# Linear attention and a Fourier feed-forward block on one core: single operations take other places in a plan's line, and the first queries are loaded ahead of the keys

## The chip, the core and the metric

The kernel runs on one core of a Trainium2 chip. The core has five engines that run side by side, each through its own queue in order: TensorE (PE in the profile) multiplies matrices out of SBUF into PSUM, VectorE (DVE) and ScalarE (ACT) read and write both memories, GpSimd (POOL) works on SBUF, and SyncE (SP) here does little but issue transfers (DMA). They wait for one another with semaphores. An instruction that waits holds up everything behind it on its engine.

The metric is the time of one execution on the device in microseconds. The kernel before takes 1024.65 us, the median of three runs between 1022.66 and 1026.61.

## The reference

Everything is fp32. B = 8 batches, H = 8 heads, S = 576 tokens, D = 64 per head, so 512 per token.

```python
kv  = einsum('bhsd,bhse->bhde', k, v)
out = einsum('bhsd,bhde->bhse', q, kv)
x   = out / sqrt(mean(out * out, -1) + 1e-6) * g_norm      # then heads side by side: (8, 576, 512)

mixed = real(fft(fft(x, axis=1), axis=2))
u  = x + mixed
un = (u - mean(u)) / sqrt(var(u) + 1e-6)                   # over the 512
out = u + maximum(un @ w_ch1, 0) @ w_ch2                   # 512 -> 2048 -> 512
```

The two weight matrices are given as 64-bit floats.

## The kernel before

**Stages.** For each batch, keys and values are multiplied (`ps_k`, line 590, copied to `kvt`), the queries are turned by matmuls against an identity (`ps_q`, lines 660 and 666, copied to `fq`), and queries times `kvt` give the attention output (`ps_o`, line 691; for batch 0 line 747, a second time with `kvg`, which is `kvt` times the gain `gb`). Squares are summed, a root gives the norm, and the rows are folded (`ab`, `xe`, `xh`, `xl`), since the real part of the Fourier transform needs only sums and differences of mirrored rows and columns. Two more products with constant matrices are the transform: `ps_f` over the sequence (lines 901 and 913, constants `cs`) and `ps_f` over the channels (line 955, constants `cd`). The result is mixed into `x`, turned (`ps_t`, line 1053) and kept as `unTh` and `unTl`.

**Precision.** A matmul at full rate takes a rounded form of fp32. So each factor is split into a high and a low part, and a product is three matmuls: high by high, low by high, high by low. The 64-bit weights are brought to this form on the chip: one ACT operation, five DVE steps and a sum (`ps_a`, `wp`, `wa`, lines 362 to 379 and 1109), then, for the first matrix, the mean over its rows by a matmul (`ps_w`, line 393), its subtraction on DVE (line 402), and the high and low parts.

**Feed-forward.** The 4608 tokens are nine blocks of 512; the 2048 inner columns are 16 parts of 128. `ps_h` (line 435) is a block times a part of the first matrix, `acc` (line 452) adds up the second product. Three parts of the weights are ready early, so blocks of the batches that are finished can start while later batches still go through the attention; partial sums go to DRAM and come back.

**What sets the order.** Each piece of work is entered in a plan with an engine, a cost in ns, a rank and what it needs. The planner walks through a modelled time: whenever an engine comes free it gives it the ready operation of lowest rank, if the buffers it asks for are free in their rings. The order in which the planner emits is the order on each engine's queue. Ranks are ten times the batch plus a stage (keys 0, queries 1, output 2, ... turns 7); feed-forward work has ranks from 1000. When nothing else is to be had, PE gets spare matmuls (`ps_s`, line 507), which multiply constants and whose result nobody reads. As long as no feed-forward work has begun, the planner also prefers them over waiting when PE has had few columns in its last 3.4 us.

Of the kernel before, what the change touches and what calls it, by code (L numbers as in the profile page):

```python
# [55 lines left out]
class Plan:  # L56
# [205 lines left out]
def kernel(  # L262
# [14 lines left out]
    nc = tc.nc  # L277
# [241 lines left out]
    def plan_dft(part, dst, src, n, r, key):  # L519
        size = src.shape[-2] * src.shape[-1]  # L520
        raw = ring("x", one, [P, 2 * DM], "draw")
        hi = dst[:, part, 0].rearrange("p t c -> p (t c)")
        lo = dst[:, part, 1].rearrange("p t c -> p (t c)")
        flat = src[part].rearrange("p t c -> p (t c)")
        ld = []
        for lo_, hi_ in ((0, n - n % 16), (n - n % 16, n)):
            if lo_ < hi_:
                ld.append(dma(
                    3 * (hi_ - lo_), r,
                    lambda lo_=lo_, hi_=hi_: nc.sync.dma_start(raw.t[lo_:hi_, :size], flat[lo_:hi_]),  # L530
                    kv_loaded, [raw],
                ))
        b = op("ACT", 950 if key == "s" else 620, r, lambda: nc.scalar.activation(hi, raw.t[:n, :size], AF.Copy), ld, [raw])
        c = op(
            "DVE", 1060 if key == "s" else 680, r,
            lambda: nc.vector.tensor_tensor(lo, raw.t[:n, :size], hi.bitcast(F32), ALU.subtract),
            [b], [raw], port=True,
        )
        dft[key, part] = c

    last_qkv = []

    def plan_kv(b):
# [7 lines left out]
        for pr in range(NPAIR):  # L551
# [3 lines left out]
            for c, src, kr in (("k", k, rest[0]), ("v", v, rest[1])):  # L555
                on = dict(eng="ACT") if b == 0 and c == "v" else {}
                start = nc.scalar.dma_start if on else nc.sync.dma_start
                if b == 0 and pr == NPAIR - 1:
                    main = Buf("h", lambda c=c: h_tile(c + "h").bitcast(F32).rearrange(
                        "p (h j d) -> p h j d", h=2, j=4  # L560
                    ))
                else:
                    main = Buf("kv", lambda c=c: qkv.tile(
                        [P, 2, 4, D], F32, name=c + "m", tag="m", bufs=RINGS["kv"]
                    ))
                ts.append(main)
                ld.append(dma(
                    256, rank(b, KV),
                    lambda main=main, src=src, hs=hs, start=start: start(
                        main.t.rearrange("p h j d -> p h (j d)"),  # L570
                        src[b, hs, : 4 * P].rearrange("h (p j) d -> p h (j d)", j=4),
                    ),
                    bufs=[main], **on,
                ))
                if pr == 0:
                    lds.append(dma(
                        128, rank(b, KV),
                        lambda kr=kr, src=src, start=start: start(
                            kr.t, src[b, :, 4 * P :].rearrange("h p d -> p h d")
                        ),  # L580
                        bufs=[kr], rate=150, **on,
                    ))
# [34 lines left out]
    def plan_q_load(b, side):  # L617
# [16 lines left out]

        ld = [dma(576, rank(b, QT), load, bufs=[qt], rate=290 if wide else 150)]
        if not side:
            ld.append(dma(
                2, rank(b, QT),
                lambda: nc.sync.dma_start(rows_of(qt.t[TR : TR + 1])[:, 0], q[b : b + 1, :, 0, :]),
                bufs=[qt],  # L640
            ))
        return qt, ld

    def plan_q(b, side, j, qt, ld):

        n = TR + 1 if side == 0 and j == 0 else TR
        fq = ring("fq", qkv, [P, NPAIR, TR + 1], "fq")
        done = []
# [31 lines left out]
    def plan_out(b, t, fqs, done, kvt, x, ss):  # L680
# [17 lines left out]

        r = rank(b, OUT)
        a = op("PE", 1500, r, mm, done, [kvt, x, ss] + pss + fqs)  # L700
        last_qkv.append(a)
        cs_, ds = [], []
        for s in range(2):
# [3 lines left out]

            c = op("ACT", 594, r - D1, og, [a], [pss[s], x])
            q_ = op(
# [11 lines left out]
            cs_.append(c)  # L721
        gs = []
        for side in range(2):
            def scale(side=side):
# [112 lines left out]
    def plan_fold(b, t, x, y_done, yp, gs, ms=None):  # L837
        n = rows[t]
        if ms and t == 0:
# [34 lines left out]
        def even(s):  # L874
            def go():
                o, a = two_of(xe), two_of(ab)
                nc.gpsimd.tensor_tensor(o[:, s], a[:, 0], a[:, 1], ALU.subtract if s else ALU.add)  # L877
# [4 lines left out]
        e = [op("POOL", 750, r, even(s), [f], [ab, xe]) for s in range(2)]  # L882
        h = op("ACT", 640, r, lambda: nc.scalar.activation(xhl.t[0][:n], two_of(xe), AF.Copy), e, [xe, xhl])

        def low():
            nc.gpsimd.tensor_tensor(
                xhl.t[1][:n], two_of(xe), xhl.t[0][:n].bitcast(F32), ALU.subtract
            )

        return xhl, op("POOL", 1270, r, low, [h], [xe, xhl]), z  # L890

# [52 lines left out]
    def plan_chn(b, t, x, pt, dones):  # L944
# [3 lines left out]
        for part in range(2):  # L948
# [126 lines left out]
    def plan_w(which, f, ring_, pool, r, after=(), r_load=None, slow=False, late_=False):  # L1075
# [19 lines left out]
        early = ring_ == "wA"  # L1095
        away = slow or early and which == 1
        a = dma(512, r if r_load is None else r_load, lambda: w_load(which, f, raw.t), after, [raw])
        d = op("ACT", 643, r, lambda: w_clear(raw.t, ps.t), [a], [raw, ps] + held, wait=SLACK if FILL <= r < 2 * FILL else 0)
# [101 lines left out]
    zeros = []  # L1200
    for b in range(B):
        begin = len(plan.ops)
        kvt, kvt_done, kv_loaded, kvg = plan_kv(b)
        xs = [ring("x", one, [P, 2 * DM], "x") for _ in range(3)]
        reds, gs, fqs = [], {}, {}
        for side in range(2):
            qt, loaded = plan_q_load(b, side)
            for j in range(3):
                fqs[side, 2 - j if side else j] = plan_q(b, side, j, qt, loaded)
        if b:  # L1210
# [9 lines left out]
        muls = {}  # L1220
        for t in (2, 1, 0) if b == 0 else range(3):
            pair = [fqs[side, t] for side in range(2)]
            if b == 0:
# [7 lines left out]
            )  # L1231
            reds += d
        y, yp = plan_y(b, ss, reds) if b else (None, None)
        if b == 0:
# [4 lines left out]
        xhl, lows = [None] * 3, [None] * 3  # L1239
        for t in (2, 1, 0) if b == 0 else range(3):  # L1240
            xhl[t], lows[t], z = plan_fold(b, t, xs[t], y, yp, gs.get(t), muls.get(t))
            zeros.append(z)
        gate_seq = muls.get(0, [])
        pt = Buf("pt", lambda: [one.tile([P, 2, 2, NS], F32R, name=f"pt{i}") for i in range(2)])
        pts = [plan_seq(b, grp, xhl, pt, lows) for grp in range(4)]
        for t in (2, 1, 0) if b == 0 else range(3):
            plan_chn(b, t, xs[t], pt, pts)
# [55 lines left out]

    for j in range(NBLK):
        plan_early(j, unTs[j], turned[j])


# [10 lines left out]
    for f in range(NA, F1):  # L1318
        for which in (1, 2):
            plan_w(which, f, "wB", lambda: wB1[0], FILL + f, [swapped], slow=(which == 1))  # L1320

    def close():
# [105 lines left out]
    def plan_late():  # L1428
        unT, unT_in = {}, {}
        for j in early[:2]:  # L1430
            unT[j], unT_in[j] = unTs[j], []
        begun = {}
# [158 lines left out]
```

## Time and profile before

| | |
|---|---|
| median of three runs | 1024.65 us |
| the profiled execution | 1019.38 us |
| its span, first to last instruction | 1017.6 us |
| mean granted TensorE clock | 0.992 |
| PE busy | 1005.8 us (99%) |
| DVE, ACT, POOL busy | 474.4, 325.6, 311.6 us |
| spare matmuls on PE | 84, 25.6 us |

The profile is of one execution. A row of the timeline gives start, length, engine, line, operation and `out<-in`; a row of the chain of waits gives start, length and what ran; both are in us from the span's start. An entry in square brackets is the engine's idle time before the row and what ended it. PE rows count each fp32 matmul of the short kinds as two instructions, so `x16` of one pass through the program may stand as `x32`. The granted clock is 1 at full speed and 0.5 at half.

### The profile page before, as it was taken

What the parts mean: (1) busy time and instruction counts of PE and PEld (TensorE: products, weight loads), DVE (VectorE), ACT (ScalarE), POOL (GpSimd) and SP (SyncE); (2) the same over time, 40 slices, a digit from 0 to 9 for tenths busy, and PEclk for the clock granted to TensorE, in tenths of its full rate; (3) what the DMA queues carried; (4) which work ended last, traced back from release to release, by engine and by line L of the source; (5) the groups of instructions that cost most, each with busy time, mean ns of one, the idle gap of its engine ahead of it and who ended that gap; (6) DMA issues with size and microseconds to landing.
All of it is one profiled execution on the core that took longest, in us unless ns stands there. A gap on an engine that the chain in (4) does not pass through costs nothing.

```text
span 1017.6 us, 15655 instructions
## 1 busy us (share of the span) xinstructions
PE 1005.8 (99%) x6208; PEld 846.9 (83%) x6208; DVE 474.4 (47%) x855; ACT 325.6 (32%) x651; POOL 311.6 (31%) x320
## 2 busy tenths in 40 slices
PE   7999999999999999999999999999999999999998
PEld 6898899889888788888888888888888888888886
DVE  3868674654676657988931313131221221311312
ACT  1566565655644433433312121121121121121110
POOL 0346976665664211224343232211030020020010
PEclk7999999999999999999999999999999999999999
DMA  9969885773435844668162524320310400500201
GB/s 245 228 188 263 210 245 166 218 214 118 172 105 186 294 167 166 226 212 299 34 243 60 189 93 156 114 93 21 142 65 11 176 21 1 186 21 0 104 1 42
DMA packets 103629, 144.95 MB, mean 142 GB/s; under 512 B 42638, under 2 KB 70338, under 8 KB 98436
## 3 DMA queue, kind: packets, MB, share of 16 engines
q1 hardware_dynamic: 94836, 127.04, 39.4%
q10 hardware_dynamic: 6800, 10.62, 2.9%
q0 software_dynamic: 1920, 6.29, 2.1%
q8 instruction: 49, 0.80, 0.3%
q14 instruction: 24, 0.20, 0.1%
HBM read 92.52 MB, written 51.40 MB: 141 GB/s over the span
## 4 chain that ended last, share of the span: by engine, by line
PE 90%; DMA 5%; DVE 3%; ACT 1%; issue 1%; ACTq 0%; SPq 0%; DVEq 0%
PE ps_h L435 37%; PE acc L452 36%; PE ps_o L691 3%; PE ps_f L955 3%; PE ps_f L901 3%; PE ps_k L590 3%; DMA vm<-in_v_dram 2%; DMA part_scr<-part 2%; PE ps_t L1053 1%; PE ps_q L666 1%; PE ps_s L507 1%; DMA raw<-in_moe_w_ch_dram 1%; PE ps_q L660 1%; DMA km<-in_k_dram 1%; PE ps_f L913 0%
## 5 line engine op out<-in xcount | busy, mean ns | idle before, releaser
L452 PE MATMUL acc<-w,hh 128*128 128x512 f32 x1152 | 357.9, 392 | 0.0
L435 PE MATMUL ps_h<-unTh,w 128*128 128x512 f32 x1152 | 356.2, 390 | 0.0
L447 DVE SCALAR_TENSOR_TENSOR hl<-ps_h,hh 128x512 fp32r<-128x512 f32 x144 | 99.2, 689 | 367.2 <-ACT hh L444 366.5
L435 PEld LDWEIGHTS ps_h<-unTh,w 128*128 128x128 f32 x1152 | 214.8, 188 | 43.8
L452 PEld LDWEIGHTS acc<-w,hh 128*128 128x128 f32 x1152 | 213.9, 188 | 43.6
L444 ACT ACTIVATE hh<-ps_h 128x512 fp32r<-128x512 f32 x144 | 86.0, 598 | 474.6 <-PE ps_h L435 459.7
L452 PE MATMUL acc<-w,hl 128*128 128x512 f32 x576 | 224.7, 390 | 0.5 <-DVE hl L447 0.4
L435 PE MATMUL ps_h<-unTl,w 128*128 128x512 f32 x576 | 224.2, 389 | 0.0
L1423 POOL TENSOR_TENSOR uu<-uu,up 128x512 f32<-128x512 f32 x36 | 45.4, 1297 | 314.4 <-DVE hl L447 228.0
L452 PEld LDWEIGHTS acc<-w,hl 128*128 128x128 f32 x576 | 108.1, 188 | 24.1 <-DVE hl L447 1.3
L435 PEld LDWEIGHTS ps_h<-unTl,w 128*128 128x128 f32 x576 | 108.1, 188 | 22.6
L726 POOL TENSOR_TENSOR x<-x,gb 96x512 f32<-96x512 f32 (+1 forms) x42 | 54.5, 1316 | 53.2 <-ACT x L706 50.5
L1131 POOL TENSOR_TENSOR w<-wap,w 128x512 fp32r<-128x512 f32 x18 | 24.1, 1342 | 92.7 <-ACT w L1126 92.6
L715 DVE TENSOR_REDUCE ss<-ps_o 96x8 f32<-96x512 f32 (+1 forms) x42 | 28.8, 687 | 34.8 <-ACT ps_o L711 29.4
L1468 DVE SCALAR_TENSOR_TENSOR uu<-acc,rs_yb,uu 128x512 f32<-128x512 f32 x36 | 25.2, 744 | 41.7 <-PE acc L452 41.7
L877 POOL TENSOR_TENSOR xe<-ab 96x256 f32<-96x256 f32 (+1 forms) x46 | 35.2, 787 | 22.4 <-DVE ab L870 21.2
L1365 POOL TENSOR_TENSOR up<-up 128x512 f32<-128x512 f32 x16 | 20.5, 1293 | 65.1 <-DMA up<-next_scr 64.9
L1065 DVE TENSOR_TENSOR unTl<-ps_t,unTh 128x384 fp32r<-128x384 f32 (+14 forms) x80 | 33.4, 481 | 8.0 <-ACT unTh L1062 8.0
L955 PE MATMUL ps_f<-cd,pt 128*96 128x258 f32 (+1 forms) x288 | 35.9, 282 | 0.0
L955 PEld LDWEIGHTS ps_f<-cd,pt 128*96 128x96 f32 (+1 forms) x288 | 34.8, 162 | 0.7
L901 PE MATMUL ps_f<-cs,xh 97*128 97x290 f32 (+1 forms) x168 | 34.3, 299 | 0.0
L691 PEld LDWEIGHTS ps_o<-kvt,fq 64*96 64x96 f32 (+1 forms) x672 | 30.7, 162 | 4.2 <-issue 3.2
(135 smaller groups left out, 1045.7 us busy)
## 6 DMA issues: line engine op xcount, KB each, us to landing
raw<-in_moe_w_ch_dram SPq DMA_DIRECT2D x32, 512.0 KB
unTh<-unT_scr SPq DMA_DIRECT2D x11, 1024.0 KB
unTl<-unT_scr SPq DMA_DIRECT2D x11, 1024.0 KB
qt<-in_q_dram SPq DMA_DIRECT2D x16, 576.0 KB
unT_scr<-unTh SPq DMA_DIRECT2D x9, 1024.0 KB
unT_scr<-unTl SPq DMA_DIRECT2D x9, 1024.0 KB
part_scr<-part ACTq DMA_DIRECT2D x36, 256.0 KB
up<-part_scr SPq DMA_DIRECT2D x36, 256.0 KB
```

The source lines that it names most:

```text
L435: nc.tensor.matmul(ps, w[c][:, kc * P : (kc + 1) * P], unT[a][:, kc, :], start=(kc == 0 and n == 0), stop=(kc == KC - 1 and n == 2),)
L444: nc.scalar.activation(hh, ps, AF.Relu)
L447: nc.vector.scalar_tensor_tensor(hl, ps, 0.0, hh.bitcast(F32), ALU.max, ALU.subtract)
L452: nc.tensor.matmul(acc, hpair[a][:, i * P : (i + 1) * P], w[c], start=(first and n == 0), stop=(last and n == 2),)
L590: nc.tensor.matmul(ps.t[s * D : (s + 1) * D, pr * D : (pr + 1) * D], km[:, s, j, :] if j < 4 else kr[:, h, :], vm[:, s, j, :] if j < 4 els ...
L691: nc.tensor.matmul(pss[s].t[:n, at : at + D], fqs[side].t[half, m, :n], kvt.t[half, m], start=True, stop=True,)
L726: nc.gpsimd.tensor_tensor(v_, v_, gb[:n].unsqueeze(1).to_broadcast([n, H, D]), ALU.mult)
L877: nc.gpsimd.tensor_tensor(o[:, s], a[:, 0], a[:, 1], ALU.subtract if s else ALU.add)
L901: nc.tensor.matmul(ps.t[:, :NS], xs[t].t[a][:n, part, ch * P : (ch + 1) * P], cs[:n, part, c, t, :], start=(idx == 0), stop=(idx == 8),)
L955: nc.tensor.matmul(ps.t[:n, :ND], pt.t[a][:, part, ch, offs[t] : offs[t] + n], cd[:, part, c, ch, :], start=(idx == 0), stop=(idx == 5),)
L1065: nc.vector.tensor_tensor(unTs[j].t[1][:, :, to], view()[:, :, lo:hi], unTs[j].t[0][:, :, to].bitcast(F32), ALU.subtract,)
L1423: lambda i=i: nc.gpsimd.tensor_tensor(us_[i].t, us_[i].t, parts[i].t, ALU.add),
```

## The change

1. A table MOVES adds an amount to the rank of 35 kinds of operation, named by function, engine, batch and tile. A negative number lets the operation go earlier, a positive one later.
2. A table MODES names 14 steps. In six outputs (`out/b/t`) the attention output is multiplied by `gb` on DVE as it leaves PSUM, four operations, in place of two ACT copies and two POOL products. In three channel mixes (`chn/b/t`) the mixed halves stay in PSUM and DVE adds them to `x`, in place of POOL. In three folds (`fold/b/t`) the sums go to a PSUM bank and DVE does them and the low part, in place of POOL. Two weight tiles (`w/1/5`, `w/1/6`) have their low part on DVE.
3. In batch 0 the queries get a lower rank than the keys, `gb` comes behind them, and the values are loaded by SP's queue instead of ACT's. Two of the six turned queries of batch 0 borrow the tiles of `pt`, which are not used until the sequence transform. Keys and values of a head pair now stand next to each other in rank.
4. The load rates in the plan's model are lower, for keys and values, queries, transform constants and weights.
5. The first weight tile's load has rank 1.5 instead of -1.

```diff
+MODES = {
+    "chn/2/1": 1,
...
+    "fold/3/1": 1,
...
+    "out/3/0": 1,
...
+    "w/1/5": 0,
+    "w/1/6": 0,
+}
+MOVES = {
...
+    "plan_q.turn/PE/1": -4,
...
+    "plan_w.<lambda>/PE/w1/0": -50,
...
+}
...
+        b, t = self.where
+        o.key = (f"{what}/{b}", f"{what}/{b}/{t}")
+        o.rank = rank + sum(MOVES.get(k, 0) for k in o.key)
...
-    i_gb = dma(32, URGENT, lambda: nc.sync.dma_start(gb, g_norm.partition_broadcast(P)))
+    i_gb = dma(32, -0.5, lambda: nc.sync.dma_start(gb, g_norm.partition_broadcast(P)))
...
-                on = dict(eng="ACT") if b == 0 and c == "v" else {}
+                on = {}
...
-                    256, rank(b, KV),
+                    256, rank(b, KV) + pr / 10,
...
-        ld = [dma(576, rank(b, QT), load, bufs=[qt], rate=290 if wide else 150)]
+        r_load = rank(b, QT) - (2 if b == 0 else 0)
+        ld = [dma(576, r_load, load, bufs=[qt], rate=230 if wide else 150)]
...
+        if b == 0 and side and j:
+            fq = View(lent, lambda t: t[j - 1].bitcast(F32).rearrange("p a c n -> p (a c n)")[
+                :, : NPAIR * (TR + 1)
+            ].rearrange("p (c n) -> p c n", c=NPAIR))
...
+            def ogg(s=s):
+                for u in range(2):
+                    nc.vector.tensor_tensor(
+                        x.t[:n].rearrange("p (u m s d) -> p u m s d", u=2, s=2, d=D)[:, u, :, s],
+                        pss[s].t[:n].rearrange("p (u m d) -> p u m d", u=2, d=D)[:, u],
+                        gb[:n].unsqueeze(1).to_broadcast([n, NPAIR, D]), ALU.mult,
+                    )
+            if merge:
+                c = op("DVE", 720, r - D1, ogg, [a, i_gb], [pss[s], x])
+            else:
+                c = op("ACT", 594, r - D1, og, [a], [pss[s], x])
...
+        quick = MODES.get(f"fold/{b}/{t}", 0)
+        eng = nc.vector if quick else nc.gpsimd
...
-        quick = b == 0 and t < 2
+        quick = MODES.get(f"chn/{b}/{t}", int(b == 0 and t < 2))
...
-                    plan_w(which, f, "wA", lambda: wA, 9 + f / 10, [], (-1, 6, 9)[f])
+                    plan_w(which, f, "wA", lambda: wA, 9 + f / 10, [], (1.5, 6, 9)[f])
```

More of the change, by code (lines that the diff above doesn't have):

```diff
@@ L42 @@
 }
+MODES = {
+    "chn/2/1": 1,
+    "chn/2/2": 1,
+    "chn/3/2": 1,
+    "fold/3/1": 1,
+    "fold/3/2": 1,
+    "fold/5/2": 1,
+    "out/3/0": 1,
+    "out/4/0": 1,
+    "out/5/1": 1,
+    "out/5/2": 1,
+    "out/6/0": 1,
+    "out/7/0": 1,
+    "w/1/5": 0,
+    "w/1/6": 0,
+}
+MOVES = {
+    "plan_chn.add_l/POOL/1": 0.5,
+    "plan_chn.add_r/POOL/0": 20,
+    "plan_chn.mix/DVE/2": -4,
+    "plan_chn.mix/DVE/2/2": -50,
+    "plan_chn.mm/PE/2/1": 1.5,
+    "plan_dft.<lambda>/DVE/0": 50,
+    "plan_early.<lambda>/ACT/e2/-": 1000,
+    "plan_early.<lambda>/PE/e3": 960,
+    "plan_early.<lambda>/PE/e7": 900,
+    "plan_early.<lambda>/PE/e7/-": 920,
+    "plan_first.<lambda>/PE/e7/-": 960,
+    "plan_fold.<lambda>/ACT/2/0": -10,
+    "plan_fold.even.go/POOL/0": 18,
+    "plan_fold.fold/DVE/1/2": -10,
+    "plan_fold.mul/DVE/2/0": 50,
+    "plan_fold.mul/DVE/7": -0.5,
+    "plan_out.mm/PE/1/0": -50,
+    "plan_out.og/ACT/1/0": -1,
+    "plan_out.og/ACT/1/1": -10,
+    "plan_q.take/ACT/2": -4,
+    "plan_q.take/ACT/7/10": 50,
+    "plan_q.turn/PE/1": -4,
+    "plan_q.turn/PE/4": -30,
+    "plan_q.turn/PE/7/10": 3.5,
+    "plan_turn.high/ACT/0/1": 12,
+    "plan_turn.high/ACT/2": -2,
+    "plan_turn.high/ACT/2/0": -9.5,
+    "plan_turn.high/ACT/2/1": -4,
+    "plan_turn.low/DVE/2/0": 30,
+    "plan_turn.low/DVE/2/1": -30,
+    "plan_turn.turn/PE/2/0": -30,
+    "plan_w.<lambda>/ACT/w2/1": 4,
+    "plan_w.<lambda>/PE/w1/0": -50,
+    "plan_w.<lambda>/PE/w1/2": 28,
+    "plan_w.hi/ACT/w1/1": -10,
+}
 class Buf:
@@ L530, in plan_dft @@
                     lambda lo_=lo_, hi_=hi_: nc.sync.dma_start(raw.t[lo_:hi_, :size], flat[lo_:hi_]),
-                    kv_loaded, [raw],
+                    kv_loaded, [raw], rate=250,
                 ))
@@ L541, with pt_buf @@
     last_qkv = []
+    def pt_buf():
+        return Buf("pt", lambda: [one.tile([P, 2, 2, NS], F32R, name=f"pt{i}") for i in range(2)])
+    lent = pt_buf()
     def plan_kv(b):
@@ L1095, in plan_w @@
         early = ring_ == "wA"
-        away = slow or early and which == 1
-        a = dma(512, r if r_load is None else r_load, lambda: w_load(which, f, raw.t), after, [raw])
+        away = not late_ and MODES.get(f"w/{which}/{f}", slow or early and which == 1) or late_
+        a = dma(
+            512, r if r_load is None else r_load, lambda: w_load(which, f, raw.t), after, [raw],
+            rate=300 if which == 1 else 345,
+        )
         d = op("ACT", 643, r, lambda: w_clear(raw.t, ps.t), [a], [raw, ps] + held, wait=SLACK if FILL <= r < 2 * FILL else 0)
@@ L1201 @@
     for b in range(B):
+        plan.where = (b, "-")
         begin = len(plan.ops)
@@ L1232 @@
             reds += d
+        plan.where = (b, "-")
         y, yp = plan_y(b, ss, reds) if b else (None, None)
@@ L1243 @@
         gate_seq = muls.get(0, [])
-        pt = Buf("pt", lambda: [one.tile([P, 2, 2, NS], F32R, name=f"pt{i}") for i in range(2)])
-        pts = [plan_seq(b, grp, xhl, pt, lows) for grp in range(4)]
+        pt = pt_buf()
+        pts = []
+        for grp in range(4):
+            plan.where = (b, grp)
+            pts.append(plan_seq(b, grp, xhl, pt, lows))
         for t in (2, 1, 0) if b == 0 else range(3):
+            plan.where = (b, t)
             plan_chn(b, t, xs[t], pt, pts)
@@ L1304 @@
     for j in range(NBLK):
+        plan.where = (f"e{j}", "-")
         plan_early(j, unTs[j], turned[j])
+    plan.where = ("-", "-")
     def swap():
@@ L1319 @@
         for which in (1, 2):
+            plan.where = (f"v{which}", f)
             plan_w(which, f, "wB", lambda: wB1[0], FILL + f, [swapped], slow=(which == 1))
+    plan.where = ("-", "-")
     def close():
```

46 lines of the change are left out of this document (32 added, 14 removed).

## The prediction

> **What bounds the kernel now.** I read the page first, then the stretches by engine, then the waits of TensorE, then the chain of waits and the timeline of the first 135 us.
>
> ```profile
> span 1017.6 us, 15655 instructions
> PE 1005.8 (99%) x6208; PEld 846.9 (83%) x6208; DVE 474.4 (47%) x855; ACT 325.6 (32%) x651; POOL 311.6 (31%) x320
> ...
> 150.00:300.00 150.00, 149.79 (x1286) 131.60 (x1285) 89.55 (x166) 85.19 (x192) 96.91 (x108) 1.00 0.53 168
> ```
>
> TensorE (PE) is busy for 99% of the span, and between 150 and 300 us it stands still for 0.21 us. (In such a row the busy times of PE, weight loads, DVE, ACT and POOL follow the length; then come the granted clock, the DMA share and GB/s.) There is nothing to win where PE is dense. But busy is not useful: the spare matmuls (`ps_s`) compute nothing, and a matmul at half clock takes twice as long. So I look for three things: waits, half clock and spares.
>
> ```profile
> PE ps_w L393 <- DVE wa L1109: 3.7, 1, 3.7
> PE ps_k L590 <- DMA vm<-in_v_dram: 1.4, 2, 0.8
> ...
> 1.64 8.40 PE L507 MATMUL ps_s<-still 128*128 128x512 f32 x28 [1.64 <-DVE still L499]
> 13.73 2.05 PE ps_w L393 x8
> 15.78 5.84 PE ps_k L590 x80
> 21.62 2.00 PE ps_s L507 x4
> 23.62 3.89 PE ps_q L660 x64
> 27.51 2.04 PE ps_s L507 x8
> 29.55 2.87 PE ps_o L747 x64
> 33.08 1.47 PE ps_q L660 x32
> 53.72 1.09 PE ps_w L393 x8
> 69.78 0.88 PE ps_k L590 x20
> ...
> 12.00:13.00 1.00, 0.00 (x0) 0.00 (x0) 0.93 (x3) 0.00 (x0) 0.00 (x0) 0.60 1.09 287
> 25.00:26.00 1.00, 1.00 (x18) 1.00 (x16) 0.97 (x2) 0.48 (x1) 0.00 (x0) 0.57 1.05 243
> ...
> 12.50 0.34 SPq L629 DMA_DIRECT2D qt<-in_q_dram  x1
> 13.86 0.33 SPq L629 DMA_DIRECT2D qt<-in_q_dram  x1
> ```
>
> The 28 spares end at 10.04. PE then waits 3.7 us for the first weight tile, whose means (`ps_w`) stand ahead of all else on its queue. The clock falls to half at about 12.2 (mean 0.60 in that microsecond) and is back at about 25.9. The first useful output (`ps_o`) starts at 29.55. What PE has done for the result by then is, at full-clock prices (the chain's last three rows), 1.09 us of `ps_w`, four key products at 0.88 and four query turns at 0.735 (1.47 for two): 7.55 us. So **22.0 us of the first 29.55 are overhead**. Data was not what it lacked at the end: the queries were asked for by 13.86, and PE came to them at 23.6.
>
> **The start.** On SP's queue, which issues the loads, before and then changed (`qt` queries, `km`/`vm`/`kr`/`vr` keys and values, `raw` FFN weights, `gb` the norm's gain):
>
> ```order
> L493 DMA gb<-in_g_norm_dram 128x64
> L359 DMA raw<-in_moe_w_ch_dram 128x4x256
> L359 DMA raw<-in_moe_w_ch_dram 128x1024
> L569 DMA km<-in_k_dram 128x2x256
> L578 DMA kr<-in_k_dram 64x8x64
> ```
>
> ```order
> L705 DMA qt<-in_q_dram 96x8x192
> L716 DMA qt<-in_q_dram 1x8x64
> L705 DMA qt<-in_q_dram 96x8x192
> L564 DMA gb<-in_g_norm_dram 128x64
> L645 DMA km<-in_k_dram 128x2x256
> L645 DMA vm<-in_v_dram 128x2x256
> L654 DMA kr<-in_k_dram 64x8x64
> L654 DMA vr<-in_v_dram 64x8x64
> ```
>
> Queries go first, and values now follow their keys instead of going out on ACT's queue. The weights move behind the last of batch 0's values. On PE, at its start, before and changed:
>
> ```order
> L507 MATMUL ps_s<-still 128x512 x28
> L393 MATMUL ps_w<-wa,mean_t 128x128 x4
> L590 MATMUL ps_k<-vm,km 64x64 x8
> L590 MATMUL ps_k<-vr,kr 64x64 x2
> L590 MATMUL ps_k<-vm,km 64x64 x8
> ```
>
> ```order
> L578 MATMUL ps_s<-still 128x512 x10
> L742 MATMUL ps_q<-ident,qt 64x97 x8
> L742 MATMUL ps_q<-ident,qt 64x96 x40
> L666 MATMUL ps_k<-vm,km 64x64 x8
> L666 MATMUL ps_k<-vr,kr 64x64 x2
> L578 MATMUL ps_s<-still 128x512 x2
> L666 MATMUL ps_k<-vm,km 64x64 x8
> ```
>
> Ten spares, all six query turns, then the four key products with 2, 4 and 4 spares between them and 4 behind; `ps_w` is gone from here. When is the data there?
>
> ```profile
> 0.00:5.00 5.00, 3.36 (x8) 2.69 (x9) 0.50 (x4) 1.49 (x2) 0.84 (x7) 1.00 0.36 111
> 5.00:15.00 10.00, 6.32 (x27) 5.07 (x27) 4.17 (x6) 0.62 (x1) 0.00 (x0) 0.86 1.06 294
> 16.00:20.00 4.00, 4.00 (x60) 3.38 (x56) 0.50 (x1) 1.16 (x2) 1.27 (x1) 0.50 1.11 224
> ...
> 1.64 1.35 PEld L507 LDWEIGHTS ps_s<-still 128*128 128x128 f32 x4 [1.64 <-DVE still L499]
> 2.66 2.46 PEld L507 LDWEIGHTS ps_s<-still 128*128 128x128 f32 x6
> ...
> 21.67 0.42 DVE L609 TENSOR_TENSOR kvg<-ps_k,gb 128x256 f32<-128x256 f32 x1 [5.16 <-PE ps_k L590]
> 22.12 0.37 ACT L601 COPY kvt<-ps_k 128x256 f32<-128x256 f32 x1 [4.43 <-DVE kvg L609]
> ```
>
> By 5.0 us 555 KB had flowed, about the first query half (576 KB); ten spares take until about 5.1 (2.66 + 2.46), so the turns begin with hardly a gap. From 16 to 20, behind the two requests for queries, the rate was 224 GB/s: the second half is there at 5.0 + 600/224 = 7.7. Keys, values and gain are 2336 KB more: at 294 GB/s the last lands at 15.6, at 224 at 18.1. I take the middle, 16.9. One key product, 0.88, and the two copies (21.62 to 22.49, 0.87) put `ps_o` at 18.7, by when 6 x 0.735 + 4 x 0.88 = 7.9 us of use are done. Overhead 10.8 in place of 22.0: **gain 11.2**, between 10.0 and 12.5 by the two rates.
>
> **The spares that stay.** Before, behind 29.55, 44 are left: nine pairs, an eight, a twelve and a six.
>
> ```profile
> 70.66 0.66 PE ps_s L507 x2
> 92.04 1.97 PE L507 MATMUL ps_s<-still 128*128 128x512 f32 x8
> 124.64 2.73 PE ps_s L507 x12
> 128.03 1.41 PE ps_s L507 x6
> ```
>
> 9 x 0.66 + 1.97 + 2.73 + 1.41 = 12.05 us, and 1.4 of waiting for values. The change has 74 spares in all, 24 of them ahead of `ps_o`; behind it 50: a sixteen (2.73 + 4 x 0.227 = 3.64), an eight, a six, three fours (0.66 + 2 x 0.227 = 1.1 each) and four pairs: 12.95. That is 0.9 more. PE's other matmuls are the same in number and shape.
>
> **New waits.** The weight steps leave DVE's idle start. On DVE, before and changed:
>
> ```order
> L369 TENSOR_SCALAR ps_a<-ps_a 128x512
> L370 TENSOR_SCALAR ps_a<-ps_a 128x512
> L373 SCALAR_TENSOR_TENSOR ps_a<-raw,ps_a 128x512
> L376 TENSOR_SCALAR wp<-ps_a 128x512
> L379 SCALAR_TENSOR_TENSOR wp<-raw,wp 128x512
> L1109 TENSOR_TENSOR wa<-ps_a,wp 128x512
> L402 TENSOR_TENSOR wa<-wa,ps_w 128x512
> L609 TENSOR_TENSOR kvg<-ps_k,gb 128x256
> ```
>
> ```order
> L685 TENSOR_TENSOR kvg<-ps_k,gb 128x256
> L440 TENSOR_SCALAR ps_a<-ps_a 128x512
> L441 TENSOR_SCALAR ps_a<-ps_a 128x512
> L444 SCALAR_TENSOR_TENSOR ps_a<-raw,ps_a 128x512
> L860 TENSOR_REDUCE ss<-ps_o 96x2x4 x2
> L872 TENSOR_SCALAR m<-ss 96x2x8
> L860 TENSOR_REDUCE ss<-ps_o 96x2x4 x2
> ```
>
> The steps now stand between the key product and batch 0's norm, and three more behind its folds.
>
> ```profile
> 29.94 2.04 DVE L536 TENSOR_TENSOR cs<-draw,cs 97x870 fp32r<-97x870 f32 x2
> 46.01 0.69 DVE L870 TENSOR_TENSOR part<-x 97x512 f32<-97x512 f32 x1
> ```
>
> Batch 0's last fold ended 17.2 us behind the start of `ps_o`, 2.04 of them the split of `cs`, which the change puts behind the folds. With `ps_o` at 18.7 it ends between 33.9 and 35.9, two weight steps (0.69 each) and `cs` later at 37.3 to 39.3. PE reaches the sequence transform that needs `cs` after six blocks of `ps_o` (about 1.45), 24 spares (5.8), two key products, three turns and `ps_w`: 18.7 + 8.7 + 5.8 + 1.76 + 2.2 + 1.09 = 38.2. The wait is 0 to 1.1; ACT is in order too, and its copies of `cs` now stand ahead of the last squares, so I allow 1.5, and 1.4 once more for values: **2.9**.
>
> **The 14 steps** (six outputs, three channel mixes and three folds of batches 2 to 7, and two weight tiles) come later than the stretch above.
>
> ```profile
> L726 POOL TENSOR_TENSOR x<-x,gb 96x512 f32<-96x512 f32 x28 | 36.6, 1324 | 11.2 <-ACT x L706 11.2
> L988 POOL TENSOR_TENSOR x<-x,pm 96x514 f32<-96x514 f32 x15 | 17.8, 1188 | 0.6 <-DVE pm L978 0.6
> L877 POOL TENSOR_TENSOR xe<-ab 96x256 f32<-96x256 f32 x32 | 24.8, 799 | 11.6 <-DVE ab L870 10.4 <-DVE x0h L1260 1.2
> L886 POOL TENSOR_TENSOR xl<-xe,xh 96x512 fp32r<-96x512 f32 x16 | 20.5, 1286 | 4.0 <-ACT xh L883 3.9
> L997 DVE TENSOR_TENSOR x<-x,ps_f 96x257 f32<-96x257 f32 x2 | 0.8, 412 | 0.0
> ```
>
> POOL loses 12 x 1.32, 6 x 1.19, 6 x 0.80, 3 x 1.29 and 2 weight splits of about 1.29: 34 us. DVE gains 24 and 12 half-width operations and 6 folds at about 0.42 and 5 full ones at about 0.69: 21 us. In 150 to 300 DVE is busy for 90 of 150 us, which hides them; each would cost up to 1.5 us if PE stood waiting for it. I count nothing. The single operations that only change place carry no work of their own either; what they can do is make PE wait or spare it a wait, and the 0.21 us of the first fence is all that could be saved there.
>
> **Sum:** 11.2 - 0.9 + 1.4 - 2.9 = 8.8 us off the span of 1017.6. The profiled execution took 1019.38 as a whole, 5.3 less than the median of the runs, 1024.65; I carry the difference over: **1016 us**.
>
> **Rivals.**
>
> *DVE becomes the bound.* It loses its start but not its work.
>
> ```profile
> 9.20:29.00 19.80, 16.11 (x167) 13.29 (x166) 9.79 (x15) 4.42 (x11) 1.27 (x1) 0.66 1.07 266
> 29.00:110.00 81.00, 79.55 (x1127) 68.51 (x1126) 67.28 (x129) 50.66 (x110) 42.77 (x50) 1.00 0.92 224
> ...
> 110.26 4.85 PE ps_f L901 x36
> ```
>
> 77.1 us of DVE work lie ahead of batch 1's sequence transform at 110.26. Begun at 17.8 and at the 83% of the second row they take until 110.7, no earlier than now. What stays is 3.5 us of spares behind that point (4.14 against one pair) and about 2 us of other work that the changed order has done by then: gain about 5, 1019.5. Against it: DVE waited for a late PE in that stretch, so 83% is no ceiling.
>
> *The clock stays half at the start.* Six turns at twice 0.735 from 5.1 end at 13.9; four key products took 5.84 at half clock, ten spares take 5.0 (2.00 for four); with the copies `ps_o` starts at 25.6, not 18.7: 1023. For it: the trace has the clock back only at 25.9, with `ps_k` ahead of it busy throughout and yet at half clock, so not all that keeps PE busy counts. Against it: the ten spares alone fill the time to 5.1, and the clock came back among turns.
>
> The Trainium skill ("TensorE: Matmul & The Clock Gate", "Part 4: PE-mode transpose") states that transposes do not count as activity for the clock. By that rule, taken to cover these turns, it would be the 1023 of this rival; by the rows, where matmuls against an identity stood on PE when the clock came back, it is the 1016. The trace cannot say more, since four spares stood just ahead of them.
>
> *Slower: PE loses the clock twice more.* One gap, 2.2 us old at 12.2, brought half clock until 25.9: the wait of 3.7 and, in the rows, 5.84 for 3.5, 2.05 for 1.09, 3.89 for 2.94 and some 0.9 of the spares, about 9 in all. Two such gaps, at the keys (8 to 17 us) and at batch 0's sequence transform (38 to 47), cost 18 for the 2.9 allowed: 1031. It decides once PE waits over 2 us in one place; I find at most 1.4 (first keys: 800 KB behind the second queries, 10.4 to 11.3, turns done at 9.9).
>
> **How the numbers follow.** My forecast has 0.60 (1011 to 1020), DVE as the bound 0.15, half clock 0.12, slower 0.09, and 0.04 goes to still larger gains, without any waits and with the keys at the faster rate. What a measurement of this kernel can tell from no change is about 0.5%, 5 us: faster means under 1019.5, slower over 1029.8. Nearly all of the forecast, half of the DVE case and the last 0.04 make faster 0.68; the rest of these two and half clock are no change, 0.23; slower keeps 0.09. The range, 1008 to 1024, takes in the DVE and half-clock cases.
>
> **What would show it.** `ps_o` of batch 0 near 19 us, no matmul of `ps_k` at half clock behind the first, PE waiting under 3 us in all behind that, and batch 1's sequence transform near 106 (110.3 less the 11.2, plus 3.8 for the spares that now lie ahead of it, 1.5 of new waits and 2 of work): each step right. Wrong: `ps_o` later than 23; a granted clock under 1.0 behind 10 us; a new row of waits of PE for DVE or POOL of over 5 us.

## The result, and the profile after

The change takes **1017.8 us** (median of 5 runs, 1015.84 to 1020.1) against 1024.78 before on the same chip (5 runs, 1022.66 to 1028.8): ratio 0.9926, interval 0.9897 to 0.9955. Faster by 7.0 us; forecast were 8.8 and a time of 1016. The profiled execution took 1016.8. It lies 1.0 below the median of its kernel, where the profiled execution of before lay 5.3 below; so the two profiles stand only 2.6 us apart. One of the runs in the tables below, 1034.84 us of the version with the tables alone, lies over 1.5% above the fastest of its kernel and is left out.

The head of the page, and the rows of TensorE's waits from the list of waits (total, times, longest, in us):

```profile
span 1015.0 us, 15608 instructions
PE 1002.3 (99%) x6198; PEld 844.0 (83%) x6198; DVE 493.6 (49%) x902; ACT 319.2 (31%) x639; POOL 278.5 (27%) x291
...
PE ps_k L666 <- DMA vm<-in_v_dram: 2.6, 5, 0.9
...
PE ps_w L469 <- DVE wap L455: 1.0, 1, 1.0
PE ps_s L578 <- DVE rs_s L880: 0.9, 1, 0.9
PE ps_q L742 <- DMA qt<-in_q_dram: 0.6, 1, 0.6
PE ps_k L666 <- DMA vr<-in_v_dram: 0.6, 1, 0.6
PE ps_s L578 <- DVE ss L860: 0.4, 1, 0.4
```

The one wait of 3.7 us for the weights is gone. In its place stand many of about 1 us or less, most of them for values (`vm`, `vr`): of batch 0 in the first 17 us, of a later batch at 76 and 78.5 us. Two rows show spares (`ps_s`) that wait themselves, for VectorE. TensorE's timeline (start, length, and in brackets the wait ahead; rows between are left out):

```profile
6.20 2.38 PE L742 MATMUL ps_q<-ident,qt 97*64 97x97 f32 x48
9.21 2.20 PE L742 MATMUL ps_q<-ident,qt 96*64 96x96 f32 x48 [0.63 <-DMA qt<-in_q_dram]
17.37 1.21 PE L578 MATMUL ps_s<-still 128*128 128x512 f32 x4
18.52 0.69 PE L666 MATMUL ps_k<-vh,kh 128*64 128x64 f32 x16
20.52 2.26 PE L843 MATMUL ps_o<-kvt,fq 64*96 64x64 f32 x48
...
33.06 0.73 PE L578 MATMUL ps_s<-still 128*128 128x512 f32 x2 [0.41 <-DVE ss L860]
34.65 2.45 PE L578 MATMUL ps_s<-still 128*128 128x512 f32 x8 [0.86 <-DVE rs_s L880]
42.96 0.52 PE L1013 MATMUL ps_f<-cs,xh 96*128 96x290 f32 x2
...
76.01 0.69 PE L666 MATMUL ps_k<-vm,km 128*64 128x64 f32 x16 [0.90 <-DMA vm<-in_v_dram]
78.52 1.12 PE L666 MATMUL ps_k<-vm,km 128*64 128x64 f32 x16 [0.89 <-DMA vm<-in_v_dram]
82.73 1.22 PE L506 MATMUL ps_h<-unTh,w 128*128 128x512 f32 x2
```

`ps_o` starts at 20.52. The last key product of batch 0, at 18.52, has no wait ahead of it: it stands behind four spares. At 78.5 a key product's first half takes 1.12 us in place of 0.69: half clock. The stretches, before and then changed:

```profile
0.00:25.00 25.00, 19.68 (x138) 15.75 (x140) 8.55 (x17) 3.64 (x6) 2.11 (x8) 0.74 0.94 245
60.00:90.00 30.00, 30.00 (x426) 26.12 (x425) 25.73 (x52) 20.49 (x46) 15.02 (x18) 1.00 0.88 247
90.00:140.00 50.00, 49.17 (x490) 43.41 (x489) 34.97 (x64) 30.48 (x71) 40.30 (x46) 1.00 0.86 210
```

```profile
0.00:25.00 25.00, 21.40 (x306) 17.25 (x306) 4.92 (x13) 7.60 (x15) 0.94 (x8) 1.00 1.01 254
60.00:90.00 30.00, 28.02 (x326) 23.87 (x326) 23.04 (x49) 16.63 (x40) 14.64 (x18) 0.89 0.96 278
90.00:140.00 50.00, 50.00 (x496) 45.18 (x494) 38.19 (x73) 32.60 (x74) 34.46 (x38) 1.00 0.77 175
```

From such rows comes a ledger of TensorE's time that serves no result: idle time (length less busy), spares (each 0.227 us, counted by stretch) and half of the time at half clock (length times one less the granted clock). In us:

| stretch | before | change | new start alone | ... with 26 spares fewer | change with 12 spares fewer |
|---|---|---|---|---|---|
| 0 to 25 | 19.1 | 9.0 | 11.5 | 11.6 | 9.2 |
| 25 to 60 | 5.1 | 8.9 | 8.7 | 8.8 | 6.5 |
| 60 to 90 | 1.8 | 8.0 | 2.7 | 2.8 | 4.3 |
| 90 to 140 | 6.7 | 0.9 | 9.1 | 8.5 | 0.9 |
| 140 to 990 | 0.9 | 1.7 | 2.6 | 5.0 | 1.7 |
| sum | 33.6 | 28.5 | 34.6 | 36.7 | 22.6 |
| span less sum | 984.0 | 986.5 | 986.3 | 986.2 | 987.0 |

The three kinds of loss account for the spans of the four versions with the new start to within 0.8 us; over all nine such versions below the rest is 985.1 to 987.5. Before lies 2.5 lower than the change. About 1.3 of that is in the counting: the 1.5 us in which TensorE stood still at half clock ahead of `ps_w` count one and a half times (0.8), and the spares ahead of the clock's first rise (at 5.37 us before, 6.58 in the change) took 0.43 us each and are priced at 0.227 (0.6 more in the change). What is left I can't place. So the start won 10.1 us, the next 65 lost 10.0 (6.2 of them between 60 and 90, where 3.3 are half clock), and 90 to 140 won 5.8.

### The profile page after: what moved, and what is told of

It reads as the page before. It is cut to its first block, busy times and chain, and to the rows that moved or that the text cites. A ratio compares the mean times of both kernels' runs of the same rounds, so it can differ in the third digit from the quotient of the medians.

```text
span 1015.0 us, 15608 instructions
## 1 busy us (share of the span) xinstructions
PE 1002.3 (99%) x6198; PEld 844.0 (83%) x6198; DVE 493.6 (49%) x902; ACT 319.2 (31%) x639; POOL 278.5 (27%) x291
## 4 chain that ended last, share of the span: by engine, by line
PE 95%; DVE 2%; DMA 2%; SPq 0%; ACT 0%; issue 0%; DVEq 0%; ACTq 0%
PE ps_h L506 39%; PE acc L523 38%; PE ps_f L1055 3%; PE ps_f L1001 3%; PE ps_o L773 3%; PE ps_k L666 2%; PE ps_t L1153 2%; DMA vm<-in_v_dram 1%; PE ps_q L748 1%; PE ps_s L578 1%; DMA qt<-in_q_dram 1%; PE ps_f L1013 0%; PE ps_q L742 0%; DVE ss L860 0%; PE ps_w L469 0%; DVE wap L450 0%
## 5 line engine op out<-in xcount | busy, mean ns | idle before, releaser
L523 PEld LDWEIGHTS acc<-w,hl 128*128 128x128 f32 x576 | 108.2, 188 | 22.6
L822 POOL TENSOR_TENSOR x<-x,gb 96x512 f32<-96x512 f32 (+1 forms) x30 | 39.6, 1332 | 34.3 <-ACT x L789 26.8
L977 POOL TENSOR_TENSOR xe<-ab 96x256 f32<-96x256 f32 (+1 forms) x40 | 30.8, 789 | 54.2 <-DVE ab L970 54.2
L1165 DVE TENSOR_TENSOR unTl<-ps_t,unTh 128x384 fp32r<-128x384 f32 (+13 forms) x80 | 34.2, 474 | 9.0 <-ACT unTh L1162 8.3
L773 PE MATMUL ps_o<-kvt,fq 64*96 64x64 f32 (+1 forms) x672 | 34.6, 254 | 0.1
```

What stands on the lines that cost most here:

```text
L523: nc.tensor.matmul(acc, hpair[a][:, i * P : (i + 1) * P], w[c], start=(first and n == 0), stop=(last and n == 2),)
L773: nc.tensor.matmul(pss[s].t[:n, at : at + D], fqs[side].t[half, m, :n], kvt.t[half, m], start=True, stop=True,)
L822: nc.gpsimd.tensor_tensor(v_, v_, gb[:n].unsqueeze(1).to_broadcast([n, H, D]), ALU.mult)
L977: eng.tensor_tensor(o[:, s], a[:, 0], a[:, 1], ALU.subtract if s else ALU.add)
L1165: nc.vector.tensor_tensor(unTs[j].t[1][:, :, to], view()[:, :, lo:hi], unTs[j].t[0][:, :, to].bitcast(F32), ALU.subtract,)
```

## Experiments

All medians follow in one table, with the mean granted clock of the runs. Before was run again beside every set: 1024.04, 1023.36 and 1021.52 us, 93 runs, clock 0.982 to 0.995. "Time x clock" is the mean over the runs of time times mean granted clock: about the time without half clock, if each us at half clock costs half a us. For before it is 1012.9 to 1013.1 in each of the three sets, so versions of different sets can be set side by side.

| version | spares | runs | median | clock | ratio (interval) | time x clock |
|---|---|---|---|---|---|---|
| before | 84 | 93 | 1023.4 | 0.982-0.995 | | 1013.0 |
| change | 74 | 5 | 1017.8 | 0.994-0.998 | 0.9926 (0.9897-0.9955) | 1013.6 |
| start_alone | 110 | 12 | 1022.71 | 0.997-1.0 | 0.9998 (0.9967-1.0028) | 1022.0 |
| tables_alone | 78 | 11 | 1026.55 | 0.981-0.995 | 1.0027 (0.9988-1.0066) | 1012.4 |
| before_fill | 100 | 12 | 1025.42 | 0.982-0.995 | 1.0012 (0.9973-1.0051) | 1013.9 |
| after_fill | 82 | 11 | 1013.71 | 0.997-1.0 | 0.990 (0.9872-0.9929) | 1012.9 |
| before_fill2 | 112 | 12 | 1022.12 | 0.992-1.0 | 0.9987 (0.9964-1.001) | 1017.4 |
| before_wlate | 88 | 12 | 1027.16 | 0.987-0.996 | 1.0046 (1.0014-1.0078) | 1017.9 |
| after_keysfirst | 74 | 9 | 1017.26 | 0.993-0.998 | 0.9934 (0.9909-0.9959) | 1010.8 |
| nomodes | 100 | 12 | 1026.52 | 0.992-1.0 | 1.0025 (0.9998-1.0051) | 1021.9 |
| nomoves | 108 | 12 | 1023.77 | 0.996-1.0 | 0.9995 (0.9963-1.0028) | 1021.8 |
| start_lean | 84 | 12 | 1024.83 | 0.993-1.0 | 1.0018 (0.9984-1.0052) | 1020.6 |
| after_gap | 62 | 6 | 1011.17 | 0.993-1.0 | 0.9891 (0.9843-0.9939) | 1010.5 |
| after_fill2 | 86 | 10 | 1014.55 | 0.998-1.0 | 0.9912 (0.9878-0.9946) | 1014.0 |

Spares are counted from the page's matmuls: 6124 in every version, and the rest. The expectations below call those of the new start alone 104; its page has 6234 matmuls, so they are 110.

**1. The two halves apart.** The change with both tables (places, and the 14 steps) empty, and the two tables on the old start:

```diff
-MODES = { "chn/2/1": 1, ... }     # start_alone
-MOVES = { "plan_chn.add_l/POOL/1": 0.5, ... }
+MODES = {}
+MOVES = {}
```

```diff
-        r_load = rank(b, QT) - (2 if b == 0 else 0)     # tables_alone: this and the other lines of the new start
+        r_load = rank(b, QT)
```

> The start alone: load order, the borrowed tiles, values on SP's queue, the lower load rates and the later first weight are kept; both tables are empty. Its order has 104 spare matmuls, 24 ahead of batch 0's ps_o like the change, 80 behind it (before 44, change 50). If the gain comes from the start, as I hold: ps_o of batch 0 near 20.6 us as in the change (before 29.55), so about 9 us are won there, and 36 more spares at 0.23 us give 8 of them back: about 1023 to 1024 in all, no gain that can be measured. If the tables make the gain by themselves: the same total, but with ps_o near 29.

> The two tables alone (14 steps and 35 moved kinds of operation) on the start of before. Its order has 78 spares, 40 ahead of ps_o as before and 38 behind it (before 44). If the gain comes from the start: ps_o near 29.5 us, 6 spares fewer make 1.4 us, about 1 us under before, which can't be told from no change. If the tables make the gain by themselves: about 1018, 7 us under before.

Neither half won anything: 0.9998 and 1.0027. The new start alone keeps the clock nearly always (0.997 to 1.0) and brings `ps_o` to 21.8 us, and yet the time is that of before; its 110 spares are 26 more, 5.9 us. The tables on the old start have 78 spares, and lose the clock: after 3.1 us of waiting for the weight tile, TensorE waits again behind `ps_o`.

```profile
32.94 0.69 PE L666 MATMUL ps_k<-vm,km 128*64 128x64 f32 x16 [2.28 <-DVE ss L860]
34.82 0.48 PE L666 MATMUL ps_k<-vr,kr 64*64 64x64 f32 x4 [1.20 <-DMA vr<-in_v_dram]
```

The clock's record then is at half from 33.8 to 61.1 us. By time x clock the tables alone (1012.4) stand with before (1013.0) and the change (1013.6), and the new start alone (1022.0) does not: it has the clock and pays in spares and waits. What the change wins is in the two halves together, not in a sum of them.

**2. Filling waits with spares.** In the kernel before 16 spares more close the wait for the weights; in the change 4 and 4 stand between the key products at 72 to 78 us:

```diff
+    EXTRA = {14: 16}                  # before_fill; after_fill: {33: 4, 34: 4}
-                for _ in range(0 if pools else 2):
+                n = 0 if pools else 2
+                if n:
+                    told[0] += 1
+                    n += EXTRA.get(told[0], 0)
+                for _ in range(n):
```

> The kernel before with 16 more spare matmuls behind the first 28, so that PE has work while it waits for the first weight's means (16 x 0.23 = 3.6 us, the length of that wait); nothing else moves. If half clock is a cost by itself: the clock stays at full from 5 us on, the key products take 3.5 us for 5.84, ps_w 1.1 for 2.05, the turns 2.9 for 3.9, ps_o starts near 24.5 and the total falls by about 5 us. If only the wait counts, since data comes late anyway: within 1 us of before.

> The changed kernel with 4 + 4 more spare matmuls around the two waits for batch 2's values at 76.0 and 78.5 us (0.9 us each, as long as PE stands still there); nothing else moves. If those two gaps cost it the clock for 6.8 us: no half clock at 78 to 85, and about 3 us less than the changed kernel, 1014 to 1015. If the clock fell for another reason, or the half clock there is hidden behind late data: the same as the changed kernel or up to 1 us more, 1018 to 1019.

In before the first wait goes and `ps_o` starts at 24.68, 4.9 us earlier, as expected; the time does not follow (1.0012). Its timeline and its stretches:

```profile
32.80 1.00 PE L597 MATMUL ps_k<-vm,km 128*64 128x64 f32 x16 [3.05 <-DVE ss L771]
...
33.00:67.00 34.00, 34.00 (x311) 29.50 (x308) 16.64 (x34) 7.64 (x19) 8.96 (x10) 0.50 0.63 152
```

PE comes 3 us too early to VectorE's sums of squares (`ss`), which the late start had hidden before, and 34 us at half clock follow. In the change 8 spares, 1.8 us of work, make the kernel 4 us faster: 1013.71. The half clock at 78 us is gone, and the mean time at half clock falls from 8.6 to 2.4 us a run. By the ratios, 0.990 against 0.9926, the intervals overlap.

That gave a **theory of the clock**: what separates the runs is time at half clock. Over the 93 runs of before, time rises by 0.54 us for each us at half clock (correlation 0.97), from 1017.27 at a mean clock of 0.995 to 1031.3 at 0.982. At one and the same clock the two kernels are equal: the eight runs of before at 0.995 took 1017.27 to 1019.25, the three of the change at 0.995 and 0.996 took 1016.8 to 1018.99.

**3. Can before be brought there by spares, or by the loads?** One version fills the second wait too (12 spares more at 28 us). One moves only the first weight tile behind the keys and queries. One puts the change's keys and values ahead of its queries again. A fourth undoes the 14 steps alone.

```diff
+    EXTRA = {14: 16, 21: 12}          # before_fill2, as in before_fill
-  plan_w(which, f, "wA", lambda: wA, 9 + f / 10, [], (-1, 6, 9)[f])
+  plan_w(which, f, "wA", lambda: wA, 9 + f / 10, [], (1.5, 6, 9)[f])   # before_wlate
-        r_load = rank(b, QT) - (2 if b == 0 else 0)
+        r_load = rank(b, QT)          # after_keysfirst
-MODES = { "chn/2/1": 1, ... }
+MODES = {}                            # nomodes
```

> The kernel before with 16 spares more behind its first 28 (which closes the wait for the first weight tile) and 12 more ahead of the query turns at about 28 us, where the version with the 16 alone then waited 3.0 us for VectorE's sums of squares and lost the clock from 33 to 67 us. Nothing else differs from before: no query is loaded earlier, no step goes to another engine. Theory 'the clock' (most of what the change wins is time at half clock that it spares): the clock stays at 1.0 behind the first wait, and the median is 1013 to 1016 us, no later than the change's 1017.8. Rival 'the start' (queries first let useful work begin 9 us earlier, and that is the gain): ps_o still starts near 25 us, 28 more spares cost 6.4 us at full clock, and the median is 1020 or more. If the clock falls at still another place, the granted clock shows it, and the run decides nothing.

> The kernel before with one number changed: the first weight tile is loaded behind the keys and the first queries in place of ahead of them; keys still come ahead of queries, no step goes to another engine. Its spares stand anew: 24 ahead of the first query turn, 88 in all. Theory 'the weight's place' (what the change wins at the start comes from not standing still for the weights, and not from the queries): no wait of 3.7 us, ps_o starts at about 21 us, and the time is within 3 us of the change's 1017.8. Rival 'queries first': the keys land late and the turns come later still, ps_o at 24 us or behind, and 1022 or more.

> The change with keys and values of batch 0 loaded ahead of its queries again; all else, the 14 steps too, is the change's. PE starts with 14 spares and the key products with spares between them, and the six turns stand behind. Theory 'order of the loads hardly matters' (the same bytes must land before ps_o either way): ps_o starts at 20.5 to 22 us, as in the change, and the time is within 3 us of 1017.8. Rival 'queries first matters': the key products are short (0.88 us each) and the loads long, so PE waits several times over 1 us for values in the first 15 us, the clock falls to half there, ps_o starts at 24 us or later, and the time is 1021 to 1026.

> The change with its 14 steps back where they were before (in none of them DVE takes them out of PSUM); the places of the single operations and the queries ahead of the keys stay. 100 spares stand in its line in place of 74, most of the 26 more from about batch 1 on. Theory 'hidden' (the prediction counted nothing for the 14 steps): the same time as the change within 2 us, if the spares stand where PE would otherwise wait. Rival 'the steps save spares': 26 x 0.227 = 5.9 us more, 1023 to 1024. Theory 'the clock': the one that has less time at half clock is the faster, and with the spares' fill the 78 to 85 us stretch at half clock (3.4 us lost in the change) may be gone, so +2.5 us net.

The second fill keeps the clock until 45.8 us; then a wait of 2.71 for values takes it for 10.2 us more. 1022.12: no better than before. The clock fell at another place, and by the condition set for that case this profile decides nothing. But the two runs at a mean clock of 1.0 took 1018.08 and 1019.27, not 1013 to 1016, so the 28 spares eat most of what the clock gives, and the 1013 of "time x clock" is not a time that filling reaches. The clock alone is not the whole answer: one has to have it without paying for it in spares.

Moving the weights alone is slightly worse than before, 1.0046, and `ps_o` starts at 24.0, not 21: the first keys' last rows (`kr`) let PE go on only at 10.05, and the clock is half from 10.3 to 17.1 and from 30.8 to 44.4. These are the numbers of the rival 'queries first'; but in the change itself the order of keys and queries hardly matters: `ps_o` at 20.57 and 1017.26 with keys first, though its profile waits 1.78 and 0.60 behind `ps_o` and is at half clock from 30.0 to 43.7 us. Why late weights suffice with the change's other loads and not with before's was not tried apart.

Undoing the 14 steps costs 8.7 us, of which 26 spares are 5.9. The prediction had counted nothing for them.

**4. Who needs the spares?** The new start alone with 26 spares fewer behind 90 us; the change without its places but with the steps; the change with 12 of its sixteen spares at 31 to 37 us left out; and 4 spares more at the start of after_fill.

```diff
+    EXTRA = {35: -2, 37: -2, 38: -2, 39: -2, 43: -2, ... 51: -2}   # start_lean
-MOVES = { "plan_chn.add_l/POOL/1": 0.5, ... }
+MOVES = {}                                                          # nomoves
+    EXTRA = {16: -2, 17: -2, 18: -2, 19: -2, 20: -2, 21: -2}        # after_gap
+    EXTRA = {5: 4, 33: 4, 34: 4}                                    # after_fill2
```

> The version with the new start alone (no new places, none of the 14 steps), with 26 of its 104 spares taken out: of the groups of 8 and 20 that stand at about 94 and 106 us two each are left, and two of the four ahead of them. The start alone saved 8 us of overhead in its first 25 us and yet was no faster than before. Theory 'the others are not ready' (what the start wins, PE gives back between 60 and 135 us, since batch 1's other engines are no earlier): PE now waits where the spares stood, 5 to 6 us in all behind 90 us, on rows of VectorE or GpSimd, perhaps with the clock at half behind it, and the time stays at 1020 to 1026. Rival 'too many spares' (nothing is late there, the planner only fills): no new wait over 2 us, and 26 x 0.227 = 5.9 us less, 1016 to 1018.

> The change with all its new places of single operations undone; the new start and the 14 steps stay. Its line has the 104 spares of the version with the start alone, at the same places. With the places and without the steps it was 1026.5; with both 1017.8; with neither 1022.7. Theory 'the steps only pay with the places' (the steps take 34 us from GpSimd, but PE stands as long as the order of the line and its spares is the old one): 1021 to 1024, as with neither. Rival 'the steps are the gain': 1018 or less, with fewer waits behind 90 us.

> The change with 12 of its sixteen spares at 31 to 37 us taken out, 4 left; all else as in the change. PE must wait there for VectorE's norm of batch 0 in any case, 2.7 us more (12 x 0.227) in place of the spares. Theory 'the clock' (spares that stand in a wait cost nothing, and what they buy is the clock): two waits of 1.5 us or more at 31 to 37, then half clock for 7 to 27 us, 3.4 to 13.7 us lost, median 1021 to 1031. Rival 'spares buy nothing there': the waits grow by 2.7 us and the spares shrink by as much, the clock stays, and the median is 1017 to 1019.

> The version of the change with 8 spares more at about 73 to 78 us, and 4 more among its first ten, ahead of the query turns. In that version the clock fell once more, from 14.9 to 18.3 us, behind a wait of 1.2 us for values; ps_o is bound by the last values there, so 4 spares (0.9 us) ahead move the turns and close that wait. Theory 'the clock': no half clock at 15, ps_o no later than 21.4, and 1.7 us less at most: median 1012 to 1014. Rival 'every spare costs its 0.227': 1014.6.

*The new start alone.* Taking 26 of its spares out does not make it faster, 1024.83 against 1022.71. The same stretch with the spares, and then without them:

```profile
90.00:140.00 50.00, 50.00 (x452) 43.44 (x451) 36.42 (x67) 28.94 (x66) 36.83 (x42) 1.00 0.74 176
```

```profile
90.00:140.00 50.00, 46.19 (x430) 40.74 (x429) 37.12 (x68) 29.29 (x66) 37.02 (x43) 0.97 0.75 184
...
PE ps_k L622 <- DMA vm<-in_v_dram: 3.1, 2, 2.3
PE ps_k L622 <- DVE w L1190: 0.4, 1, 0.4
PE ps_k L622 <- DMA vr<-in_v_dram: 0.3, 1, 0.3
```

3.8 us of waiting and 3.4 us at half clock stand where 26 spares stood. PE got there too early, and the spares were the price of that; the theory expected 5 to 6 us, and VectorE or GpSimd as the cause, while 3.4 of the 3.8 are loads of values. The longest, 2.3 us, is for values that SyncE issued at 104.61, after it had stood 3.0 us until `ps_o` (L729) let a tile go.

*Places and steps.* Steps without places: 1023.77, as with neither (1022.71, 1.1 apart, with intervals of about 3). Places without steps: 1026.52. Both: 1017.8. Without the places the 14 steps take 32 us from POOL (312.0 to 280.0 busy), and yet 108 of the 110 spares stay in PE's line; with them it is 74. The spares between 90 and 140 us are 40 with neither, 40 with the steps, 18 with the places (and 14 more behind 140), 4 with both.

*The sixteen.* Here both theories were wrong: 1011.17, faster than the change by 6.6 (5.2 by the means of 6 and 5 runs) and than anything else. Its timeline, where the change waited 0.41 and 0.86:

```profile
31.24 1.20 PE L585 MATMUL ps_s<-still 128*128 128x512 f32 x4
32.37 0.69 PE L673 MATMUL ps_k<-vm,km 128*64 128x64 f32 x16
33.83 0.33 PE L673 MATMUL ps_k<-vr,kr 64*64 64x64 f32 x4 [0.78 <-DMA vr<-in_v_dram]
...
38.75 1.13 PE L464 MATMUL ps_w<-wa,mean_t 128*128 128x128 f32 x8 [0.33 <-DVE wa L1219]
39.63 0.89 PE L1020 MATMUL ps_f<-cs,xh 96*128 96x290 f32 x2
...
41.64 0.40 PE L1020 MATMUL ps_f<-cs,xh 96*128 96x290 f32 x1 [0.45 <-DVE cs L614]
```

No row of PE waiting for VectorE's norm is left there: the key products that follow never needed it. It was the spares that waited, since a spare writes a PSUM bank, and the bank had to come free from batch 0's norm first. The 12 cost 2.7 us of work and 1.27 of waiting, and hid no more than the waits of 0.78, 0.33 and 0.45 that now show: the sequence transform (`ps_f`) starts 3.3 us earlier. In this profile the clock stays at 1.0 from 7.2 us to the last 2.3 us of the span; over its six runs it was 0.993 to 1.0, and the slowest, 1018.28, is the one at 0.993. The two waits for values at 73 to 79 us became 0.18 and 1.21, where they were 0.90 and 0.89. That this is why the clock held there is likely, not shown.

*Four more at the start.* 1014.55 against 1013.71: nothing won. The half clock at 15 us came all the same (15.2 to 18.6), behind a wait of 1.3 us for the same values.

## Why the prediction was right, and where it was not

**The start: right, mis-sized by 1.8.** Forecast was `ps_o` at 18.7 and overhead 10.8; it is 20.52, and 12.6 with 7.9 us of use. The gain of the start is 9.4, not 11.2 (and below the 10.0 of its lower bound). Two terms were too small. The landings were late: the second half of the queries at 9.2 for 7.7, the last values at 17.7 for 16.9 (by the trace's record of their transfer, 17.66). And PE was not free when they landed: the last key product began behind four spares at 18.52, and four more spares stood between it and `ps_o`.

**The clock at the start: right.** It is at 1.0 from 6.58 to 78.27 us, through 48 and 48 turns with nothing else on PE from 6.2 to 11.4. The rival with half clock is out. The rule of the Trainium skill ("TensorE: Matmul & The Clock Gate", "Part 4: PE-mode transpose"), taken to cover these turns, does not agree with that record; they are plain matmuls against an identity, the clock held, and the measurement decides. In five other versions with the new start the clock did fall once, for 3.41 us at 14.9 to 15.5, behind waits for values that follow the turns.

**New waits: too small, and in the wrong places.** 2.9 us allowed, 4.5 measured by the rows behind `ps_o` (0.41, 0.86, 0.90, 0.89 and 1.0 for a weight tile at 479 us are the large ones). The forecast put them at the sequence transform, which waited for nothing, being late itself (42.96 for 38.2): the spares ahead of it waited for their banks. With 12 of these spares out, it comes at 39.63 and does wait for `cs`, 0.45.

**Half clock behind the start: the step that failed.** The prediction priced a lost clock only in the rival "PE loses the clock twice more", "once PE waits over 2 us in one place", and gave the forecast none. In the profile two waits of 0.9 us, 1.6 us of work apart, took it for 6.83 us; by the mean clock of the five runs, the last stretch of the span included, it is 8.6 us, 4.3 us of time. And before has 20.6 us on the mean, not the 15.5 of its one profile (13.65 and 1.9 at the end). So that term was too small on both sides, and the measured gain is nearly all made of it: half of 20.6 less 8.6 is 6.0, of 7.0 against the five runs of before and 5.6 against the 93. What the changed start took out of the first 25 us beyond the clock came back as spares and waits until 90 us.

**The sum: near by luck.** It was added up from one profile, for a span 8.8 us shorter; between the two profiles it is 2.6 shorter. The start was worth 1.8 less, the waits cost 0.9 more (4.5 less the 2.1 of before, for 2.9 less 1.4), and half clock took 3.4 that had no term: 8.8 less these is 2.7. The forecast then carried over the 5.3 us between profile and median, and of these the change has only 1.0. So 1016 came near 1017.8 because before's other runs lose the clock for longer than its profile does, which the prediction did not know. Of its own signs, `ps_o` near 19 us was nearly met (20.52); the others were not: a key product at half clock (78.52), 4.5 us of waits, the transform of batch 1 at 113.99 for 106, and, named as a sign of being wrong, a clock under 1.0 behind 10 us.

**"I count nothing" for the 14 steps and the places: right for the steps alone, wrong for both together.** The work moved as forecast (POOL 33.1 us less busy for 34, DVE 19.2 more for 21). On the new start the steps alone change 1.1 us; the places alone came out 3.8 slower, with intervals that overlap. With the new start they are worth 4.9 us together (1022.71 to 1017.8), by sparing 36 spares, and 8.4 by time x clock. The prediction did count the spares of the whole change, 74, and so had that in its sum without saying so: the "start" was priced with a line of spares that only the tables make possible. So the sum was one for both halves together, and no half alone gives any of it.

**DVE as the bound.** Its mechanism was there for the new start alone: PE ahead of the others, and the gain given back as spares between 90 and 140 us (40 against 26). The stretch is named rightly, and the culprit only in part: mostly loads of values, as the version with 26 fewer shows. With the tables on, 4 spares are left there. Batch 1's sequence transform, forecast near 106 and 110.26 before, began at:

```profile
113.99 4.86 PE ps_f L1001 x36
```

Later than before, and yet the kernel is faster, since behind it only four spares follow where 18 did: the instant of one operation said nothing of the end.

## What to carry to other kernels

Where a dense engine loses its clock by standing still, keep a ledger by stretch of idle time, filler and half clock before pricing an edit: a gain at the start is real only if what follows is ready, else it turns into filler or waits. Filler is work: place it only in a wait that the next real instruction has, check what the filler itself waits for, and try taking it out, which here won 6.6 us where adding it elsewhere won 4.1 (the two are not clearly apart). Read the clock of many runs and not of one profile: half-clock time was nearly all of the spread of 14 us.

## What the runs showed of the hardware

- Half clock came in pieces of 3.41, 6.83, 10.24, 13.65, 27.31 and 34.13 us, all multiples of 3.41 (apart from the last piece of a profile, which the end of the program cuts off). Behind the wait of 3.05 us ahead of 32.80 (16 spares more in before) it lasted 34 us with PE busy for 34.00 of 34.00; that PE is busy does not bring it back at once. What does is open.
- What takes it is idle time summed over a step of 3.41 us, and no long wait is needed. Counted in such steps from the first rise in each record, the first 140 us of the 14 profiles have 17 falls, each at the end of a step in which PE stood for 1.20 to 3.05 us in all. Of the 481 other steps at full clock two had as much, 1.21 and 1.29. So two waits of 0.9 us took it at 78.27 (1.54 us of idle in that step), and one of 1.21 did not (at 75.95, in the version with 12 spares fewer): a step ended at 75.48 and cut that wait in two.
- A spare that fills a wait can itself be held by its PSUM bank (0.41 and 0.86 us).
- One execution is a poor witness: before's 93 runs cover 1017.27 to 1031.3 us, and the mean granted clock orders them.
